# Two attention blocks with backward: a recurrence that keeps its state in one tile and stores wide rows, and a backward recurrence with regrouped heads, a fourth PSUM buffer and copies on ScalarE

## The chip, the cores and the metric

The kernel runs on one core of one Trainium2 chip. The metric is device time in microseconds (us). The kernel before took 9784.7 us (median of 4 runs, 9771.98 to 9796.26).

Engine names are as in the profile: PE is TensorE, PEld its weight loads, DVE VectorE, ACT ScalarE, POOL GpSimd, SP the queue that issues most DMAs. "Granted clock" (PEclk) is the share of the full TensorE clock that the throttle let through. PSUM tiles are the ones that matmuls write; an "evacuation" copies such a tile out on DVE or ACT.

## The reference

The forward function mixes two attention blocks over 2048 tokens of width 512; the kernel returns its output and the gradients for 11 of its inputs.

```python
g = sigmoid((x * gate_w).sum(-1, keepdims=True))
a = A(x)         # 32 heads of 16, shared k and v, full softmax
b = B(x)         # the part that this change touches
out = g * a + (1 - g) * b

# B: a recurrence over 64 segments of 32 tokens with 8 memory rows
mem = mem0
for s in range(64):
    h = concat([mem, x[s*32:(s+1)*32]])        # 40 rows
    q, k, v = h @ Wq, h @ Wk, h @ Wv           # 32 heads of 128
    p = softmax(mask(q @ k.T * scale))         # 40 x 40 in each head
    o = (p @ v) @ Wo
    mem = o[:8]                                # what the next segment needs
    outs.append(o[8:])
# reference(): jax.vjp of all this for grad_out
```

## The kernel before

One program does, in this order: attention A forward and backward (untouched); the B forward recurrence ("forward"); the combination with the gate; the B backward recurrence ("backward"); and four passes that accumulate the weight gradients of Wq, Wk, Wv and Wo ("dW", passes q, k, v, o). The two recurrences cannot overlap their steps: step s+1 needs the memory rows (or their gradient) of step s.

The forward step, cut:

```python
for s_ in range(NS):                                     # 64 steps
    hT = sp.tile([P, 4, TB], BF16, name="hT")            # TB = 40 = 32 tokens + 8 memory rows
    nc.vector.tensor_copy(out=hT[:, :, 0:LB], in_=xT[:, :, s_ * LB:(s_ + 1) * LB])
    nc.vector.tensor_copy(out=hT[:, :, LB:TB], in_=memT_cur[:])
    qT_s = project("qT", Wq, 0); kT_s = project("kT", Wk, 1)   # 128 matmuls each, ps_proj
    # ... scores, softmax, vT, transposes ...
    nc.scalar.dma_start(PT_all[s_], PT[:])               # nothing reads PT_all
    # ... o of this step into columns slot3*40.. of oT3 [128, 32 heads, 128] ...
    oT_s = oT3[:, :, slot3 * TB:(slot3 + 1) * TB]
    nc.sync.dma_start(oT_all[s_], oT_s)                  # 128 x 32 runs of 80 B
    # ps_m = Wo^T o for the 8 memory rows (128 matmuls, ps_memT)
    nc.vector.tensor_copy(out=memT_next[:], in_=ps_m[:]) # copied again into hT in the next step
```

The backward step, cut. `R` copies are evacuations of 128x128 transposes; heads alternate between partitions 0-39 (even) and 64-103 (odd):

```python
psA = pool("bb_psA", bufs=3, PSUM); psB = pool("bb_psB", bufs=2, PSUM)   # psC: three tags, one bank each
# load qT_s, kT_s into [128, 32, 64] (80 B runs), vT_s, P2 twice; transpose d(out) into dobT
doT_s = Wo^T dob                                # 128 matmuls ps_doT, three evacuations
for gi, (h0, h1) in enumerate(HGRPS):           # heads 0-11, 12-23, 24-31
    # ps_dP = doT . vT, head h at partition 64 * (h % 2)
    for par in range(2):                        # 4 DVE operations on 6 (or 4) heads
        prod = ps_dP * P2; delta = sum(prod); tsub = ps_dP - delta; dS2 = tsub * SCALE_B * P2
do_R = transposes_R2(doT_s)                     # two 128x1024 copies, both on DVE
dvT_s = grad_T(do_R, P2)                        # per group: two half tiles of psA, evacuated on ACT and DVE
dh_part(0, WvT, dvT_s)                          # 128 matmuls, ps_dhT
k_R = transposes_R2(kT_s); q_R = transposes_R2(qT_s)
# dST = transposes of dS2; dkT = grad_T(q_R, dS2); dh_part(1, WkT); dqT = grad_T(k_R, dST); dh_part(2, WqT)
nc.scalar.copy(out=dh_f[:], in_=ps_dh[:, 0])                                   # the "tail"
nc.vector.tensor_tensor(out=dh_f[:], in0=dh_f[:], in1=ps_dh[:, 1], op=ALU.add)
nc.vector.tensor_tensor(out=dhT_s[:], in0=dh_f[:], in1=ps_dh[:, 2], op=ALU.add)
nc.vector.tensor_copy(out=dmemT_new[:], in_=dhT_s[:, :, LB:TB])   # copied again into dobT next step
```

The framework orders each engine's instructions when it builds the program, so the source order above is not the order on DVE or PE.

The softmax here doesn't subtract the row's maximum and nothing guards it: scores larger than these inputs give would overflow.

## Time and profile before

| stage | from - to, us | length | per step (64) | granted clock |
|---|---|---|---|---|
| attention A | 0 - 4148 | 4148 | | 0.96 |
| forward | 4148 - 6030 | 1882 | 29.4 | 0.76 |
| combine, weights | 6030 - 6219 | 189 | | 0.69 |
| backward | 6219 - 8364 | 2145 | 33.5 | 0.76 |
| dW | 8364 - 9776 | 1412 | | 0.84 |

The table is read from the busy times of stretches of the trace, kernel before. Columns: stretch in us from the start, its length, busy us of each engine with its number of instructions, then granted clock, mean busy share of the DMA engines, GB/s.

```profile
core 0: us, PE busy (x) PEld busy (x) DVE busy (x) ACT busy (x) POOL busy (x), PEclk, DMA share, GB/s
0.00:4148.00 4148.00, 3596.12 (x93133) 3253.67 (x93134) 2891.06 (x7880) 2655.93 (x5199) 296.81 (x533) 0.96 0.40 141
4148.00:6030.00 1882.00, 1562.08 (x46923) 1481.02 (x46924) 662.68 (x1170) 446.39 (x768) 8.40 (x21) 0.76 0.50 56
6030.00:6219.00 189.00, 55.80 (x959) 48.08 (x957) 61.96 (x146) 36.23 (x56) 14.99 (x26) 0.69 0.60 167
6219.00:8364.00 2145.00, 1722.45 (x46584) 1556.83 (x46584) 1237.08 (x3197) 269.80 (x768) 200.29 (x311) 0.76 0.40 70
8364.00:9776.00 1412.00, 991.51 (x25348) 954.07 (x25348) 840.00 (x1234) 238.64 (x233) 351.01 (x608) 0.84 1.03 86
```

Forward first. The waits of PE in the forward stage, kernel before: who waited for whom, us in total, times, longest.

```profile
engine line waited for: us in total, times, longest us
PE ps_proj L52 <- issue: 236.3, 103, 5.7
PE ps_oT L668 <- DVE oT L673: 15.0, 20, 0.7
...
```

"issue" means that PE waited for nothing that the profile shows: no semaphore. A loss of 236 us to nothing is worth asking about. The same view of stretches, in steps of 1 us over one forward step (same columns as above), kernel before; the oT_all store was issued at 4225.88:

```profile
4228.00:4229.00 1.00, 1.00 (x43) 1.00 (x41) 0.00 (x0) 0.00 (x0) 0.00 (x0) 0.50 1.66 78
4229.00:4230.00 1.00, 1.00 (x40) 1.00 (x38) 0.10 (x1) 0.00 (x0) 0.00 (x0) 0.50 2.18 22
4230.00:4231.00 1.00, 1.00 (x30) 1.00 (x28) 0.27 (x2) 0.00 (x0) 0.00 (x0) 0.50 1.76 36
4231.00:4232.00 1.00, 1.00 (x36) 1.00 (x33) 0.00 (x0) 0.00 (x0) 0.00 (x0) 0.50 1.91 39
4232.00:4233.00 1.00, 1.00 (x36) 1.00 (x33) 0.00 (x0) 0.56 (x1) 0.00 (x0) 0.50 1.72 20
...
4234.00:4235.00 1.00, 0.11 (x2) 0.03 (x2) 0.66 (x1) 0.00 (x0) 0.00 (x0) 1.00 0.27 3
4235.00:4236.00 1.00, 0.00 (x0) 0.00 (x0) 0.00 (x0) 0.00 (x0) 0.00 (x0) 1.00 0.19 3
4236.00:4237.00 1.00, 0.49 (x16) 0.49 (x16) 0.00 (x0) 0.00 (x0) 0.00 (x0) 0.77 0.04 1
```

The last two columns tell it. For some 6 us the DMA engines are fully busy (the share adds the time of packets, and passes 1 here) while they move only 20 to 80 GB/s: that is the store in runs of 80 B. At 4234 to 4236.5 PE stands still. The queue list of the page, kernel before, has a queue of kind "instruction" (packets, MB, share):

```profile
q8 instruction: 1668, 27.33, 1.3%
```

That is 16.4 KB a packet. The Trainium skill, page "Runtime: NRT & Kernel Launch", section "Instruction fetch mechanics", says that an engine's instructions come by DMA in blocks of 16 KiB, and calls the cost mostly hidden. The packet size agrees. PE has 426969 instructions in this trace, 256 for each of the 1668 packets.

Backward next. The chain of work that ended last, in order of time, kernel before (start, us, what, times). One step's DVE part runs from the first `prod` to WvT's matmuls:

```profile
7000.62 0.41 DVE prod L876
...
7010.73 0.34 DVE prod L876
7011.09 0.33 DVE dS L884
7011.44 0.32 DVE delta L878
7011.78 0.42 DVE dvT_s L816
...
7012.24 0.29 PE ps_dT L894 x4
7012.53 4.06 PE ps_dhT L52 x115
```

From 7000.62 to 7012.46 (where PE starts the 115 matmuls) are 11.84 us in which DVE is busy for 11.12 us and PE for 6.86. The chain passes through softmax operations (prod, delta, tsub, dS) until the last evacuation of dvT on DVE, then PE takes over. Groups of instructions by shape in the backward stage, kernel before (count, busy us, mean ns, idle before):

```profile
L876 DVE TENSOR_TENSOR prod<-ps_dP,P 40x240 f32<-40x240 f32 x256 | 103.8, 405 | 12.3 <-PE ps_dP L868 4.2
L876 DVE TENSOR_TENSOR prod<-ps_dP,P 40x160 f32<-40x160 f32 x128 | 41.3, 323 | 4.0
L828 DVE COPY do_R<-ps_tr 128x1024 bf16<-128x1024 bf16 x128 | 87.4, 683 | 2.0
```

240 elements take 405 ns, 160 take 323, and an R copy 683.

### The profile page before, as it was taken

The numbers are of one execution on the slowest core, as the hardware profiler recorded it, in microseconds if no ns is written. First come the engines' busy times: TensorE is split into PE (matmuls) and PEld (weight loads), VectorE is DVE, ScalarE is ACT, GpSimd is POOL, SyncE is SP. The second block draws the span as 40 slices with busy tenths as digits, with TensorE's granted clock in tenths as the row PEclk, the third lists the DMA queues.
The fourth block names the chain that finished last, engine by engine and source line by source line (L and its number), as shares of the span: only waits on it lengthen the run. The fifth ranks groups of instructions, "written<-read, shape, count | busy, mean of one in ns | idle before, by whom it ended". The sixth has DMA issues, their size and how long they took to land.

```text
span 9776.5 us, 461191 instructions
## 1 busy us (share of the span) xinstructions
PE 7928.0 (81%) x212940; PEld 7293.7 (75%) x212940; DVE 5692.8 (58%) x13627; ACT 3647.0 (37%) x7023; POOL 871.5 (9%) x1498
## 2 busy tenths in 40 slices
PE   5999998799999998488888886678887887477677
PEld 5778877788888898377777875577777777477667
DVE  2555555599999998033333333455555555466556
ACT  3666666477777776022222221211111111111111
POOL 0000000000000000000000000000000000122221
PEclk9999999999999999577777777777777777689888
DMA  2444444244444443244554545534343433999996
GB/s 88 166 166 167 168 166 166 100 140 141 141 141 142 141 143 118 99 57 56 55 57 57 57 56 92 117 69 69 69 71 69 72 70 67 106 84 71 105 87 61
DMA packets 2184111, 994.17 MB, mean 102 GB/s; under 512 B 1926144, under 2 KB 1970336, under 8 KB 2179104
## 3 DMA queue, kind: packets, MB, share of 16 engines
q1 hardware_dynamic: 1312320, 561.59, 30.8%
q10 hardware_dynamic: 772832, 108.85, 10.4%
q0 software_dynamic: 97024, 294.21, 8.9%
q8 instruction: 1668, 27.33, 1.3%
q14 instruction: 267, 2.19, 0.1%
HBM read 494.58 MB, written 464.59 MB: 98 GB/s over the span
## 4 chain that ended last, share of the span: by engine, by line
PE 46%; DVE 15%; issue 7%; ACT 6%; DMA 4%; SPq 2%; ACTq 1%; POOL 0%; another core or an unknown queue 0%; DVEq 0%; POOLq 0%
PE ps_dhT L52 8%; PE ps_proj L52 7%; PE ps_acc L1074 4%; PE ps_T L421 3%; ACT dsub L410 3%; PE ps_VK L417 2%; PE ps_ob L575 2%; PE ps_memT L680 2%; PE ps_doT L52 2%; PE ps_dP L68 2%; PE ps_acco L1062 2%; DVE dST L423 2%; SPq L1017 2%; DVE prod L876 2%; DVE delta L878 1%
## 5 line engine op out<-in xcount | busy, mean ns | idle before, releaser
L410 ACT ACTIVATE dsub<-ps_dP,delta 128x512 bf16<-128x512 f32 x2048 | 1296.7, 686 | 128.8 <-DVE dS L412 64.0
L275 ACT ACTIVATE E_t<-ps_S 128x1024 bf16<-128x1024 f32 x1024 | 1039.1, 1020 | 556.9 <-PE ps_S L68 555.6
L68 PE MATMUL ps_dP<-VT16x,dOTg 128*128 128x57 bf16 (+1 forms) x18432 | 929.6, 190 | 50.5 <-ACT dsub L410 50.1
L281 DVE COPY ET<-ps_T 128x1024 bf16<-128x1024 bf16 x1024 | 708.2, 692 | 432.3 <-PE ps_T L279 432.3
L423 DVE COPY dST<-ps_T 128x512 bf16<-128x512 bf16 x2048 | 863.5, 422 | 42.7 <-PE ps_T L421 41.9
L421 PE MATMUL ps_T<-ident,dS 128*128 128x128 bf16 x8192 | 786.9, 218 | 0.0
L279 PE MATMUL ps_T<-ident,E_t 128*128 128x128 bf16 x8192 | 713.8, 220 | 76.9 <-ACT E_t L275 75.3
L68 PEld LDWEIGHTS <-dOTg 128*128 128x128 bf16 x18432 | 722.5, 97 | 68.5 <-issue 67.3
L412 DVE TENSOR_TENSOR dS<-dsub,E_b 128x512 bf16<-128x512 bf16 x2048 | 770.5, 418 | 0.5 <-ACT dsub L410 0.4
L1074 PE MATMUL ps_acc<-R,hr 120*128 120x68 bf16 (+1 forms) x16896 | 612.6, 198 | 125.6 <-issue 120.0
L415 PE MATMUL ps_VK<-dOs_R,E_b 128*128 128x16 bf16 x8192 | 707.0, 170 | 0.7 <-DVE dKacc L429 0.2
L68 PE MATMUL ps_S<-KT16x,QTg 128*128 128x57 bf16 (+1 forms) x18432 | 701.0, 190 | 0.0
L1074 PEld LDWEIGHTS <-hr 120*128 120x128 bf16 x16896 | 588.0, 102 | 139.8 <-issue 133.2
L417 PE MATMUL ps_VK<-Qs_R,dS 128*128 128x16 bf16 x8192 | 665.4, 170 | 30.2
L68 PEld LDWEIGHTS <-QTg 128*128 128x128 bf16 x18432 | 629.3, 98 | 0.0
L279 PEld LDWEIGHTS <-E_t 128*128 128x128 bf16 x8192 | 466.4, 97 | 171.5 <-ACT E_t L275 115.3
L415 PEld LDWEIGHTS <-E_b 128*128 128x128 bf16 x8192 | 560.2, 96 | 42.6 <-issue 0.2
L417 PEld LDWEIGHTS <-dS 128*128 128x128 bf16 x8192 | 503.4, 96 | 70.4 <-DVE dS L412 70.1
L1037 ACT COPY R<-ps_tr 128x1024 bf16<-128x1024 bf16 x176 | 175.7, 1013 | 947.7 <-PE ps_tr L1032 727.8
L426 PE MATMUL ps_dQ<-Ka_R,dST 128*128 128x16 bf16 x8192 | 515.2, 171 | 1.1 <-DVE dST L423 0.8
L421 PEld LDWEIGHTS <-dS 128*128 128x128 bf16 x8192 | 475.2, 96 | 0.1
L283 PE MATMUL ps_o<-Va_R,ET 128*128 128x16 bf16 x8192 | 367.8, 171 | 75.3 <-DVE ET L281 68.0
(256 smaller groups left out, 14598.0 us busy)
## 6 DMA issues: line engine op xcount, KB each, us to landing
E_all<-E_t SPq DMA_DIRECT2D x256, 512.0 KB
E_all<-E_t POOLq DMA_DIRECT2D x256, 512.0 KB, 2.9
E_b<-E_all SPq DMA_DIRECT2D x256, 512.0 KB
E_b<-E_all POOLq DMA_DIRECT2D x256, 512.0 KB, 3.7
qT_all<-qT_s SPq DMA_DIRECT2D x64, 320.0 KB
kT_all<-kT_s ACTq DMA_DIRECT2D x64, 320.0 KB
vT_all<-vT_s SPq DMA_DIRECT2D x64, 320.0 KB
oT_all<-oT SPq DMA_DIRECT2D x64, 320.0 KB
```

The lines of the kernel that those rows point to most:

```text
L52: nc.tensor.matmul(out, lhsT=lhsT, rhs=rhs, start=(j == 0), stop=(j == last), **kw)
L68: nc.tensor.matmul(out[:, pos:pos + n], lhsT=lhsT, rhs=rhs[:, pos:pos + n], start=(j == 0), stop=(j == last), **kw)
L275: nc.scalar.activation(E_kh, ps_S[:], ACT.Exp, scale=SCALE_A, accum_out=l_kh[:])
L279: nc.tensor.transpose(ps_T[:, kb, :], E_kh[:, kb * P:(kb + 1) * P], ident[:])
L281: nc.vector.tensor_copy(out=ET[:], in_=ps_T[:])
L410: nc.scalar.activation(dsub[:], ps_dP[:], ACT.Identity, bias=delta[:, qt, h:h + 1])
L412: nc.vector.tensor_tensor(out=dS[:], in0=dsub[:], in1=E_t[:, c0:c0 + SUBW], op=ALU.mult)
L415: nc.tensor.matmul(ps_VK[:, 0, kk, :], lhsT=E_t[:, c0 + kb * P:c0 + (kb + 1) * P], rhs=dOs_R[:, qt, h * DA:(h + 1) * DA], start=True, stop ...
L417: nc.tensor.matmul(ps_VK[:, 1, kk, :], lhsT=dS[:, kb * P:(kb + 1) * P], rhs=Qs_R[:, qt, h * DA:(h + 1) * DA], start=True, stop=True)
L421: nc.tensor.transpose(ps_T[:, kb, :], dS[:, kb * P:(kb + 1) * P], ident[:])
L423: nc.vector.tensor_copy(out=dST[:], in_=ps_T[:])
L1074: nc.tensor.matmul(ps[:, pos:pos + n], lhsT=Hs[ci][:, cc * P:(cc + 1) * P], rhs=Rs[ci][0:KCH * TB, hc * D + pos:hc * D + pos + n], start=( ...
```

## The change

It aims at three things: small DMA packets (the oT_all store, its loads in dW, a dead PT_all store), copies between steps, and the backward's DVE chain. The diff, cut to its core:

```diff
@@ forward
-    oT_all = dram.tile([NSEG, P, HB, TB], ...)
+    oT_all = dram.tile([(NSEG + 2) // 3, P, HB, P], ...)
-    memT_cur -> copied into hT each step
+    hT_next: ps_memT is evacuated straight into the next step's hT
-        nc.scalar.dma_start(PT_all[s_], PT[:])
-        nc.sync.dma_start(oT_all[s_], oT_s)
         if slot3 == 2 or s_ == NS - 1:
+            nc.sync.dma_start(oT_all[s_ // 3], oT3[:])       # 1 MB in 8 KB rows, every third step
@@ backward
-    psA bufs=3
+    psA bufs=4        # ps_dbT and ps_dhR moved to other tags
+    # heads 0-11 and 24-27 at partitions 0-39, 12-23 and 28-31 at 64-103
+    GSUB = {0: [(0, 12, 0)], 1: [(12, 24, 64)], 2: [(24, 28, 0), (28, 32, 64)]}
     transposes_R2:
-            nc.vector.tensor_copy(out=dstR[...hg...], in_=ps_t[:])
+            if hg == 0: nc.vector.tensor_copy(...)
+            else:       nc.scalar.copy(...)
-        nc.sync.dma_start(qT_s[:, :, 0:TB], qT_all[s_]); nc.scalar.dma_start(kT_s[:, :, 0:TB], kT_all[s_])
+        four DMAs each for q and k, by head block, on both queues
     softmax backward, grad_T, dST:
-        for par in range(2): ...            # 24 DVE operations, six dvT tiles
+        for (hlo, hhi, b) in GSUB[gi]: ...  # 16 DVE operations, four dvT tiles
     tail:
-        ACT copy, two DVE adds, two DVE copies
+        nc.vector.tensor_reduce(out=dh_f[:], in_=ps_dh.rearrange("p m cc t -> p cc t m"), axis=AX.X, op=ALU.add)
+        nc.vector.tensor_copy(out=dobT_next[:, :, LB:TB], in_=dh_f[:, :, LB:TB])
@@ dW
+                if m == "o": one dma_start(T3[:], oT_all[ch[0] // 3])   # in place of three with 80 B runs
```

More of the change, by code (lines that the diff above doesn't have):

```diff
@@ L526, in phase_B_fwd @@
     vT_all = dram.tile([NSEG, P, HB, TB], BF16, name="vT_all")
-    oT_all = dram.tile([NSEG, P, HB, TB], BF16, name="oT_all")
-    PT_all = dram.tile([NSEG, TB, HB, TB], BF16, name="PT_all")
+    oT_all = dram.tile([(NSEG + 2) // 3, P, HB, P], BF16, name="oT_all")
     P_all = dram.tile([NSEG, TB, HB, TB], BF16, name="P_all")
@@ L550, in phase_B_fwd @@
     psf1 = octx.enter_context(tc.tile_pool(name="b_ps1", bufs=1, space=bass.MemoryType.PSUM))
-    memT_cur = sp.tile([P, 4, MB], BF16, name="memT_cur")
-    nc.sync.dma_start(memT_cur[:], memT_all[0])
+    hT_next = sp.tile([P, 4, TB], BF16, name="hT")
+    nc.sync.dma_start(hT_next[:, :, LB:TB], memT_all[0])
     ob_queue = []
@@ L598, in phase_B_fwd @@
     for s_ in range(NS):
-        hT = sp.tile([P, 4, TB], BF16, name="hT")
+        hT = hT_next
         nc.vector.tensor_copy(out=hT[:, :, 0:LB], in_=xT[:, :, s_ * LB:(s_ + 1) * LB])
-        nc.vector.tensor_copy(out=hT[:, :, LB:TB], in_=memT_cur[:])
         def project(wname, W, eng_off):
@@ L681, in phase_B_fwd @@
                                  start=(h == 0), stop=(h == HB - 1))
-        memT_next = sp.tile([P, 4, MB], BF16, name="memT_cur")
-        nc.vector.tensor_copy(out=memT_next[:], in_=ps_m[:])
-        nc.scalar.dma_start(memT_all[s_ + 1], memT_next[:])
-        memT_cur = memT_next
+        hT_next = sp.tile([P, 4, TB], BF16, name="hT")
+        nc.vector.tensor_copy(out=hT_next[:, :, LB:TB], in_=ps_m[:])
         if slot3 == 2 or s_ == NS - 1:
@@ L692, in phase_B_fwd @@
     octx.close()
-    return dict(qT_all=qT_all, kT_all=kT_all, vT_all=vT_all, oT_all=oT_all, PT_all=PT_all,
+    return dict(qT_all=qT_all, kT_all=kT_all, vT_all=vT_all, oT_all=oT_all,
                 P_all=P_all, memT_all=memT_all, memR_all=memR_all, b_hbm=b_hbm)
@@ L755, in phase_B_bwd @@
     qT_all, kT_all, vT_all, oT_all = bst["qT_all"], bst["kT_all"], bst["vT_all"], bst["oT_all"]
-    P_all, PT_all, memR_all = bst["P_all"], bst["PT_all"], bst["memR_all"]
+    P_all, memR_all = bst["P_all"], bst["memR_all"]
     db_hbm = cst_["db_hbm"]
@@ L801, in phase_B_bwd @@
     rp = octx.enter_context(tc.tile_pool(name="bb_rp", bufs=3, side="right"))
-    psA = octx.enter_context(tc.tile_pool(name="bb_psA", bufs=3, space=bass.MemoryType.PSUM))
+    psA = octx.enter_context(tc.tile_pool(name="bb_psA", bufs=4, space=bass.MemoryType.PSUM))
     psB = octx.enter_context(tc.tile_pool(name="bb_psB", bufs=2, space=bass.MemoryType.PSUM))
     psC = octx.enter_context(tc.tile_pool(name="bb_psC", bufs=1, space=bass.MemoryType.PSUM))
-    dmemT_cur = sp.tile([P, 4, MB], BF16, name="dmemT_cur")
-    nc.vector.memset(dmemT_cur[:], 0.0)
+    dobT_next = sp.tile([P, 4, TB], BF16, name="dobT")
+    nc.vector.memset(dobT_next[:, :, LB:TB], 0.0)
     zr = sp1.tile([MB, D], BF16, name="zr")
@@ L818, in phase_B_bwd, with hbase, hpair @@
     TPAD = 64
+    def hbase(h):
+        return 0 if (h < 12 or 24 <= h < 28) else 64
+    def hpair(h):
+        if h < 12:
+            return h, 0
+        if h < 24:
+            return h - 12, 1
+        if h < 28:
+            return 12 + (h - 24), 0
+        return 12 + (h - 28), 1
+    PAIR_BLOCKS = [((slice(0, 12), 0), (0, 12)), ((slice(0, 12), 1), (12, 24)),
+                   ((slice(12, 16), 0), (24, 28)), ((slice(12, 16), 1), (28, 32))]
+    GSUB = {0: [(0, 12, 0)], 1: [(12, 24, 64)], 2: [(24, 28, 0), (28, 32, 64)]}
     def transposes_R2(srcTp, name):
@@ L825, in transposes_R2 @@
                 pr = hg * 8 + j
-                nc.tensor.transpose(ps_t[:, j, :], srcTp[:, 2 * pr:2 * pr + 2, :].rearrange("e a t -> e (a t)"),
-                                    ident[:])
-            nc.vector.tensor_copy(out=dstR[:, hg * 8:(hg + 1) * 8, :], in_=ps_t[:])
+                nc.tensor.transpose(ps_t[:, j, :], srcTp[:, pr, :, :].rearrange("e a t -> e (a t)"), ident[:])
+            if hg == 0:
+                nc.vector.tensor_copy(out=dstR[:, hg * 8:(hg + 1) * 8, :], in_=ps_t[:])
+            else:
+                nc.scalar.copy(out=dstR[:, hg * 8:(hg + 1) * 8, :], in_=ps_t[:])
         return dstR
@@ L832, in phase_B_bwd @@
         s_ = NS - 1 - si
-        qT_s = ld.tile([P, HB, TPAD], BF16, name="qT_s")
-        kT_s = ld.tile([P, HB, TPAD], BF16, name="kT_s")
+        qT_s = ld.tile([P, HB // 2, 2, TPAD], BF16, name="qT_s")
+        kT_s = ld.tile([P, HB // 2, 2, TPAD], BF16, name="kT_s")
         vT_s = ld.tile([P, HB, TB], BF16, name="vT_s")
-        nc.gpsimd.memset(qT_s[:, :, TB:TPAD], 0.0)
-        nc.gpsimd.memset(kT_s[:, :, TB:TPAD], 0.0)
-        nc.sync.dma_start(qT_s[:, :, 0:TB], qT_all[s_])
-        nc.scalar.dma_start(kT_s[:, :, 0:TB], kT_all[s_])
+        nc.gpsimd.memset(qT_s[:, :, :, TB:TPAD], 0.0)
+        nc.gpsimd.memset(kT_s[:, :, :, TB:TPAD], 0.0)
+        for bi, ((psl, slot), (hlo, hhi)) in enumerate(PAIR_BLOCKS):
+            eng = nc.sync if bi % 2 == 0 else nc.scalar
+            eng.dma_start(qT_s[:, psl, slot, 0:TB], qT_all[s_][:, hlo:hhi, :])
+            eng.dma_start(kT_s[:, psl, slot, 0:TB], kT_all[s_][:, hlo:hhi, :])
         nc.sync.dma_start(vT_s[:], vT_all[s_])
@@ L846, in phase_B_bwd @@
         nc.sync.dma_start(drow[pb:pb + LB, :], db_hbm[s_ * LB:(s_ + 1) * LB, :])
-        ps_db = psC.tile([P, 4, TB], BF16, name="ps_dbT", tag="dbT")
+        ps_db = psC.tile([P, 4, TB], BF16, name="ps_dbT", tag="m1")
         for cc in range(4):
@@ L850, in phase_B_bwd @@
                                 ident[pb:pb + LB, pb:pb + LB], tile_position=(pb, 0))
-        dobT = sp.tile([P, 4, TB], BF16, name="dobT")
+        dobT = dobT_next
         nc.vector.tensor_copy(out=dobT[:, :, 0:LB], in_=ps_db[:, :, 0:LB])
-        nc.vector.tensor_copy(out=dobT[:, :, LB:TB], in_=dmemT_cur[:])
-        doT_s = sp.tile([P, HB, TPAD], BF16, name="doT_s")
-        nc.gpsimd.memset(doT_s[:, :, TB:TPAD], 0.0)
+        doT_s = sp.tile([P, HB // 2, 2, TPAD], BF16, name="doT_s")
+        nc.gpsimd.memset(doT_s[:, :, :, TB:TPAD], 0.0)
         for gi, (h0, h1) in enumerate(HGRPS):
@@ L859, in phase_B_bwd, with doT_h @@
                 mm_acc(nc, ps[:, h - h0, :], [(WoT[:, cc, h * EB:(h + 1) * EB], dobT[:, cc, :]) for cc in range(4)])
-            evac(gi, doT_s[:, h0:h1, 0:TB], ps[:, 0:h1 - h0, :])
+            for k, (hlo, hhi, b) in enumerate(GSUB[gi]):
+                psl, slot = hpair(hlo)[0], hpair(hlo)[1]
+                evac(gi + k, doT_s[:, psl:psl + (hhi - hlo), slot, 0:TB], ps[:, hlo - h0:hhi - h0, :])
+        def doT_h(h):
+            pr, sl = hpair(h)
+            return doT_s[:, pr, sl, 0:TB]
         delta = sp.tile([P, HB], F32, name="delta")
@@ L863, in phase_B_bwd @@
         for gi, (h0, h1) in enumerate(HGRPS):
-            ng = h1 - h0
             ps = psA.tile([P, 12, TB], F32, name="ps_dP", tag="p12")
             for h in range(h0, h1):
-                b = 64 * (h % 2)
-                nc.tensor.matmul(ps[b:b + TB, h - h0, :], lhsT=doT_s[:, h, 0:TB], rhs=vT_s[:, h, :],
+                b = hbase(h)
+                nc.tensor.matmul(ps[b:b + TB, h - h0, :], lhsT=doT_h(h), rhs=vT_s[:, h, :],
                                  start=True, stop=True, tile_position=(0, b))
-            for par in range(2):
-                b = 64 * par
-                hs = slice(h0 + par, h1, 2)
-                ss = slice(par, ng, 2)
-                npar = len(range(h0 + par, h1, 2))
-                prod = sp1.tile([P, 6, TB], F32, name="prod")
-                nc.vector.tensor_tensor(out=prod[b:b + TB, 0:npar, :], in0=ps[b:b + TB, ss, :],
-                                        in1=P2[b:b + TB, hs, :], op=ALU.mult)
-                nc.vector.tensor_reduce(out=delta[b:b + TB, hs], in_=prod[b:b + TB, 0:npar, :], axis=AX.X,
+            for (hlo, hhi, b) in GSUB[gi]:
+                nh = hhi - hlo
+                s0 = hlo - h0
+                prod = sp1.tile([P, 12, TB], F32, name="prod")
+                nc.vector.tensor_tensor(out=prod[b:b + TB, 0:nh, :], in0=ps[b:b + TB, s0:s0 + nh, :],
+                                        in1=P2[b:b + TB, hlo:hhi, :], op=ALU.mult)
+                nc.vector.tensor_reduce(out=delta[b:b + TB, hlo:hhi], in_=prod[b:b + TB, 0:nh, :], axis=AX.X,
@@ L879, in phase_B_bwd @@
                                         op=ALU.add)
-                tsub = sp1.tile([P, 6, TB], F32, name="tsub")
-                nc.vector.tensor_tensor(out=tsub[b:b + TB, 0:npar, :], in0=ps[b:b + TB, ss, :],
-                                        in1=delta[b:b + TB, hs].unsqueeze(2).to_broadcast([TB, npar, TB]),
+                tsub = sp1.tile([P, 12, TB], F32, name="tsub")
+                nc.vector.tensor_tensor(out=tsub[b:b + TB, 0:nh, :], in0=ps[b:b + TB, s0:s0 + nh, :],
+                                        in1=delta[b:b + TB, hlo:hhi].unsqueeze(2).to_broadcast([TB, nh, TB]),
@@ L883, in phase_B_bwd, with grad_T @@
                                         op=ALU.subtract)
-                nc.vector.scalar_tensor_tensor(out=dS2[b:b + TB, hs, :], in0=tsub[b:b + TB, 0:npar, :],
-                                               scalar=SCALE_B, in1=P2[b:b + TB, hs, :],
+                nc.vector.scalar_tensor_tensor(out=dS2[b:b + TB, hlo:hhi, :], in0=tsub[b:b + TB, 0:nh, :],
+                                               scalar=SCALE_B, in1=P2[b:b + TB, hlo:hhi, :],
                                                op0=ALU.mult, op1=ALU.mult)
-        def grad_T(wname, lhsR2, rhs2, out_all):
+        def grad_T(wname, lhsR2, rhs2, out_all, groups=None):
@@ L888, in grad_T @@
             dst = sp.tile([P, HB, TB], BF16, name=f"{wname}_s", tag=wname)
             for gi, (h0, h1) in enumerate(HGRPS):
-                ps_par = [psA.tile([P, 12, TB], F32, name=f"ps_dT{par}", tag="p12") for par in range(2)]
-                for h in range(h0, h1):
-                    par = h % 2
-                    b = 64 * par
-                    nc.tensor.matmul(ps_par[par][:, (h - h0) // 2, :], lhsT=lhsR2[b:b + TB, h // 2, :],
-                                     rhs=rhs2[b:b + TB, h, :], start=True, stop=True, tile_position=(b, 0))
@@ L896, in grad_T @@
-                for par in range(2):
-                    npar = len(range(h0 + par, h1, 2))
-                    evac(gi + 1 + par, dst[:, h0 + par:h1:2, :], ps_par[par][:, 0:npar, :])
+                subs = GSUB[gi]
+                pss = [psA.tile([P, 12, TB], F32, name=f"ps_dT{k}", tag="p12") for k in range(len(subs))]
+                for k, (hlo, hhi, b) in enumerate(subs):
+                    for h in range(hlo, hhi):
+                        pr, _ = hpair(h)
+                        nc.tensor.matmul(pss[k][:, h - hlo, :], lhsT=lhsR2[b:b + TB, pr, :],
+                                         rhs=rhs2[b:b + TB, h, :], start=True, stop=True, tile_position=(b, 0))
@@ L899, in grad_T @@
+                for k, (hlo, hhi, b) in enumerate(subs):
+                    evac(gi + 1 + k, dst[:, hlo:hhi, :], pss[k][:, 0:hhi - hlo, :])
             nc.sync.dma_start(out_all[s_], dst[:])
@@ L913, in phase_B_bwd @@
         dST = sp1.tile([P, HB, TB], BF16, name="dST")
-        for hg in range(2):
-            ps_par = [psB.tile([P, 8, 64], BF16, name=f"ps_dST{par}", tag="tr") for par in range(2)]
-            for j in range(16):
-                h = hg * 16 + j
-                par = h % 2
-                b = 64 * par
-                nc.tensor.transpose(ps_par[par][b:b + TB, j // 2, 0:TB], dS2[b:b + TB, h, :],
-                                    ident[b:b + TB, b:b + TB], tile_position=(b, b))
-            for par in range(2):
-                b = 64 * par
-                nc.vector.tensor_copy(out=dST[b:b + TB, hg * 16 + par:(hg + 1) * 16:2, :],
-                                      in_=ps_par[par][b:b + TB, 0:8, 0:TB])
+        for gi, (h0, h1) in enumerate(HGRPS):
+            subs = GSUB[gi]
+            pss = [psB.tile([P, 12, 64], BF16, name=f"ps_dST{k}", tag="tr") for k in range(len(subs))]
+            for k, (hlo, hhi, b) in enumerate(subs):
+                for h in range(hlo, hhi):
+                    nc.tensor.transpose(pss[k][b:b + TB, h - hlo, 0:TB], dS2[b:b + TB, h, :],
+                                        ident[b:b + TB, b:b + TB], tile_position=(b, b))
+            for k, (hlo, hhi, b) in enumerate(subs):
+                nc.vector.tensor_copy(out=dST[b:b + TB, hlo:hhi, :], in_=pss[k][b:b + TB, 0:hhi - hlo, 0:TB])
         dkT_s = grad_T("dkT", q_R, dS2, dkT_all)
@@ L930, in phase_B_bwd @@
         dh_f = sp.tile([P, 4, TB], F32, name="dh_f")
-        nc.scalar.copy(out=dh_f[:], in_=ps_dh[:, 0])
-        nc.vector.tensor_tensor(out=dh_f[:], in0=dh_f[:], in1=ps_dh[:, 1], op=ALU.add)
+        nc.vector.tensor_reduce(out=dh_f[:], in_=ps_dh[:].rearrange("p m cc t -> p cc t m"), axis=AX.X,
+                                op=ALU.add)
+        dobT_next = sp.tile([P, 4, TB], BF16, name="dobT")
+        nc.vector.tensor_copy(out=dobT_next[:, :, LB:TB], in_=dh_f[:, :, LB:TB])
         dhT_s = sp.tile([P, 4, TB], BF16, name="dhT_s")
-        nc.vector.tensor_tensor(out=dhT_s[:], in0=dh_f[:], in1=ps_dh[:, 2], op=ALU.add)
-        dmemT_new = sp.tile([P, 4, MB], BF16, name="dmemT_cur")
-        nc.vector.tensor_copy(out=dmemT_new[:], in_=dhT_s[:, :, LB:TB])
-        dmemT_cur = dmemT_new
-        ps_r = psC.tile([TB, D], BF16, name="ps_dhR", tag="misc")
+        nc.scalar.copy(out=dhT_s[:], in_=dh_f[:])
+        ps_r = psB.tile([TB, D], BF16, name="ps_dhR", tag="tr")
         for cc in range(4):
@@ L1014, in issue_loads @@
                 T3 = ldp.tile([P, HB, P], BF16, name="T3")
+                if m == "o":
+                    (nc.sync if ci % 2 == 0 else nc.scalar).dma_start(T3[:], oT_all[ch[0] // 3])
+                    T3s.append(T3)
+                    continue
                 for j, st_ in enumerate(ch):
```

## The prediction

> **What bounds it now.** The timeline's 9776 us: attention A to 4148 (untouched); B forward 4148-6030 (1882 us, 64 steps of 29.3); combine and weights to 6219; B backward 6219-8366 (2147 us, 64 steps of 33.5); four dW passes to 9776 (q, k, v, o).
> Forward is a serial PE chain. The waits table gives PE 236 us idle before ps_proj with "issue" as releaser, 103 times, 3.7 us a step. In 1-us windows the oT_all store (4096 runs of 80 B) lasts about 7 us at DMA share near 1.9 but 20-40 GB/s, then PE stands for 2-5 us inside ps_proj. The Trainium skill, "Runtime: NRT & Kernel Launch", Instruction fetch mechanics, says instructions come by DMA in 16 KiB blocks; the queue table agrees (1668 "instruction" packets, 27.3 MB, 16.4 KB each). I read the stalls as instructions delayed behind the store. After them the granted clock is often 0.5 (36 matmuls/us, against 47).
> Backward alternates: for about 12 us DVE is the chain (24 softmax-backward operations of 0.32-0.40 us, three R copies of 0.69, dvT evacuations), then about 17 us of PE, then a 1.5 us tail (ACT copy, two adds, two copies) before ps_doT.
> dW is limited by 80 B loads (DMA share 1.66) and their stalls (PE "issue" 148 us).
>
> **Changes, costed.**
> Forward: the store becomes 8 KB rows every third step: the 3.7 us should go. Copy hT L601: 0.2 us. Better clock: 0.3 us, an estimate. About 4 us x 64 = -250 us (200 to 310).
> Backward: DVE: 24 operations become 16. From 240 elements = 0.40 us and 160 = 0.32, I estimate 480 = 0.66, so 9.0 us becomes 7.8, plus 8 hops of 0.03; half of the R copies go to ACT (one or two within the chain); an extra doT copy is 0.3. Net -2 us. Tail: one reduce (0.66, estimated) and one copy (0.19) against 1.5: -0.5. Against: heads no longer alternate row groups. ps_dT runs alternating at about 20 ns each; forward's ps_oT, same shape, one row group, at 28-38. The skill's "TensorE: Matmul & The Clock Gate", Part 3 (The mechanism), says weight loads overlap matmuls only when the row group differs, which fits. 96 matmuls: +1 to 1.5 us of PE, some 0.9 on the path, dP included. The last dvT tile still waits for the last tsub despite a fourth psA buffer, so WvT's matmuls stay behind the DVE chain. The q/k loads keep 80 B packets, in eight DMAs. Net -1.6 us a step, -100 us (-220 to +30).
> dW: only pass o changes. It takes 329 us from its first transpose (9447); without DMA limits, 7.3 supers of 31 us, start and output make about 265: -65. Its loads also delay the end of pass v (ACT held 46 us behind them): -30. Together -95 us (-50 to -130).
>
> Sum about -445: **9335 us, 80% range 9180 to 9500**. Chances: faster by over 2% 0.96, within 2% 0.035, slower 0.005.
>
> **What would show it.** Forward step 25-25.5 us; "issue" before ps_proj under 40 us. Backward step 31-32.5; softmax operations of 480 elements near 0.66; ps_dT dearer per matmul. Pass o about 265 us; passes q and k unchanged.
>
> **What would make it wrong.** Stalls not caused by the store; q and k loads bursting together and starving PE in backward; the scheduled order on ACT or DVE letting WvT's matmuls start earlier (up to 4 us a step) or holding evacuations behind DMA waits.

## The result

| | before | after |
|---|---|---|
| median, us | 9788.0 (13 runs) | 9057.4 (8 runs) |
| ratio, 95% interval | | 0.9252 [0.9242, 0.9261] |
| forward, us | 1882 | 1546 |
| backward, us | 2145 | 1842 |
| dW, us | 1412 | 1338 |

A ratio is the mean time of one kernel's runs over the mean of the other's of the same rounds, so it is not quite the ratio of the medians quoted. The kernel gained 731 us where 450 had been forecast; the measured time lies below the predicted range.

The stretches, kernel after (columns as before):

```profile
core 0: us, PE busy (x) PEld busy (x) DVE busy (x) ACT busy (x) POOL busy (x), PEclk, DMA share, GB/s
0.00:4149.00 4149.00, 3594.06 (x93132) 3251.54 (x93132) 2890.90 (x7879) 2655.91 (x5199) 296.80 (x533) 0.96 0.40 141
4149.00:5695.00 1546.00, 1475.22 (x46899) 1407.51 (x46900) 650.93 (x1106) 446.50 (x768) 8.39 (x21) 0.84 0.18 65
5695.00:5875.00 180.00, 53.92 (x989) 46.27 (x987) 61.79 (x146) 36.23 (x56) 14.95 (x26) 0.71 0.60 175
5875.00:7717.00 1842.00, 1580.16 (x46584) 1465.38 (x46580) 1014.39 (x2240) 420.62 (x767) 196.90 (x311) 0.86 0.50 81
7717.00:9055.00 1338.00, 989.96 (x25348) 954.62 (x25348) 840.56 (x1233) 239.47 (x233) 342.88 (x586) 0.84 0.88 93
```

The waits of PE in the forward stage, kernel after:

```profile
...
PE ps_proj L52 <- issue: 6.0, 16, 0.7
...
```

The store now, in 1-us stretches, kernel after; it was issued at 4723.12:

```profile
4724.00:4725.00 1.00, 1.00 (x43) 1.00 (x41) 0.00 (x0) 0.00 (x0) 0.00 (x0) 0.50 1.07 426
4725.00:4726.00 1.00, 1.00 (x44) 1.00 (x42) 0.00 (x0) 0.00 (x0) 0.00 (x0) 0.50 0.99 393
4726.00:4727.00 1.00, 1.00 (x34) 1.00 (x32) 0.29 (x2) 0.00 (x0) 0.00 (x0) 0.50 0.39 156
4727.00:4728.00 1.00, 1.00 (x35) 1.00 (x33) 0.00 (x0) 0.00 (x0) 0.00 (x0) 0.50 0.08 33
```

One MB in rows of 8 KB passes in under 3 us at up to 426 GB/s, and PE stays at 1.00. The chain of one backward step, kernel after:

```profile
6719.29 0.65 DVE prod L893
...
6725.24 0.33 DVE prod L893
6725.58 0.67 DVE dS L901
6726.27 0.31 DVE delta L895
6726.59 0.24 DVE dvT_s L811
...
6726.87 3.14 PE ps_dhT L52 x100
```

From 6719.29 to 6726.87 are 7.58 us in place of 11.84 (the chain's view ends with 100 of a run of 104). The two runs are not the same matmuls: before's 115 begin with the 14th of WvT's 128, after's 104 with the 25th. Counted alike, at the last 104, the start moved from 12.34 to 7.58 us after the first prod (medians of the 64 steps, counted in the traces), by 4.8 us, and the whole step became 4.7 us shorter. The groups, kernel after:

```profile
L893 DVE TENSOR_TENSOR prod<-ps_dP,P 40x480 f32<-40x480 f32 x128 | 83.3, 651 | 3.1 <-PE ps_dP L887 1.0
L893 DVE TENSOR_TENSOR prod<-ps_dP,P 40x160 f32<-40x160 f32 x128 | 41.2, 322 | 4.0
L840 ACT COPY do_R<-ps_tr 128x1024 bf16<-128x1024 bf16 x64 | 64.8, 1012 | 112.6 <-PE ps_tr L836 112.6
L838 DVE COPY do_R<-ps_tr 128x1024 bf16<-128x1024 bf16 x64 | 43.1, 673 | 0.0
```

480 elements take 651 ns; the prediction had estimated 660. The durations were right. What was wrong was which of them lie ahead of WvT's matmuls, as the experiments show.

### The profile page after: what moved, and what is told of

Same layout as the page of the kernel before. It is cut to its first block, busy times and chain, and to the rows that moved or that the text cites. A ratio compares the mean times of both kernels' runs of the same rounds, so it can differ in the third digit from the quotient of the medians.

```text
span 9055.7 us, 460371 instructions
## 1 busy us (share of the span) xinstructions
PE 7693.3 (85%) x212940; PEld 7125.3 (79%) x212940; DVE 5458.6 (60%) x12603; ACT 3798.7 (42%) x7023; POOL 859.9 (9%) x1476
## 4 chain that ended last, share of the span: by engine, by line
PE 62%; DVE 12%; ACT 11%; issue 6%; DMA 5%; SPq 2%; ACTq 1%; POOL 0%; DVEq 0%; POOLq 0%
PE ps_dhT L52 8%; PE ps_proj L52 7%; PE ps_T L279 7%; PE ps_acc L1092 5%; ACT E_t L275 4%; PE ps_T L421 3%; PE ps_S L68 3%; ACT dsub L410 3%; PE ps_VK L417 3%; PE ps_doT L52 2%; PE ps_memT L676 2%; PE ps_ob L574 2%; PE ps_dP L68 2%; DVE dST L423 2%; PE ps_acco L1080 2%
## 5 line engine op out<-in xcount | busy, mean ns | idle before, releaser
L1092 PE MATMUL ps_acc<-R,hr 120*128 120x68 bf16 (+1 forms) x16896 | 625.5, 200 | 106.5 <-issue 100.6
```

What stands on the lines that cost most here:

```text
L1092: nc.tensor.matmul(ps[:, pos:pos + n], lhsT=Hs[ci][:, cc * P:(cc + 1) * P], rhs=Rs[ci][0:KCH * TB, hc * D + pos:hc * D + pos + n], start=( ...
```

## The experiments

All 14 results were correct against the reference. "Stage" times are read from the profiled run of each kernel between the same instructions: forward from the first ps_proj to the last ps_memT, backward from the first ps_doT to the last dh_f. They compare kernels across calls better than totals do: in the third call the kernel before itself ran at 9716.41 us, where it took 9775 to 9787 in the others. The same backward took 1831 to 1842 us in four kernels (bwd_only, after_80B, after, after_again), so a stage difference of under some 12 us says nothing.

My theories were: in the forward the 80 B store starves PE; in the backward a fourth PSUM buffer lets WvT's matmuls start early. The rival for the forward was the saved copies; for the backward, the copies on ACT or the wider operations.

### Do the stages add up?

`fwd_only` is the kernel before with the forward and dW of after; `bwd_only` is the kernel before with the backward of after.

> Before with the forward and the dW pass of after, backward as before. If the three stages add up: forward 1882 to about 1547 us, dW 1410 to about 1340, so 9788 - 410 = about 9375 us (9350 to 9400), and the backward stays at 2147 us. If the stages lean on each other (for example, a backward that gains because the forward left something better), it is over 9430.

> Before with the backward of after alone. Additive: backward 2147 to about 1843 us, so 9788 - 303 = about 9485 us (9460 to 9510), forward still 1882 us with about 230 us of PE 'issue' before ps_proj. Rival, that part of the backward's gain came from the forward or from HBM traffic that the forward no longer makes: over 9550.

Measured: fwd_only 9363.27 us, ratio 0.9574, forward 1544, backward 2143. bwd_only 9459.36 us, ratio 0.9676, forward 1869, backward 1831. The two gains, 0.0426 and 0.0324, sum to 0.0750, against 0.0748 for the whole change. The stages are independent, and can be studied one by one.

### The store alone

`store_only` is the kernel before with only this:

```diff
-    oT_all = dram.tile([NSEG, P, HB, TB], ...)
+    oT_all = dram.tile([(NSEG + 2) // 3, P, HB, P], ...)
-        nc.sync.dma_start(oT_all[s_], oT_s)
+            nc.sync.dma_start(oT_all[s_ // 3], oT3[:])      # every third step; dW reads it so
```

> Before with nothing changed but the oT_all store (22 of 1 MB in 8 KB rows in place of 64 of 80 B runs) and its loads in dW; memT copy, PT_all store, backward as before. Theory, that the 80 B store starved PE of instructions and the stalls also pulled the granted clock down: nearly all of the forward's and dW's gain, about 9395 us (9370 to 9420), 'issue' before ps_proj under 20 us, forward clock about 0.84. Rival, that the saved copies and the PT_all store carry a good part: 9500 or more.

Measured: 9389.55 us, ratio 0.9596; forward 1569 us, "issue" before ps_proj 3.3 us, forward clock 0.84, PE busy 1483 us against 1562. The theory holds: 313 of the forward's 336 us come from the store. 233 us of them are the standing time; some 79 us more are PE busy time, for the same matmuls at a higher clock. The saved copies and the PT_all store are the remaining 23 us or so (1569 against 1546).

### The store put back

`after_80B` is the kernel after with one dead store a step into a scratch tensor that nothing reads:

```diff
+        nc.sync.dma_start(oT_scr[s_], oT_s)       # 80 B runs, [NSEG, P, HB, TB]
```

> After plus one dead store a step in the forward: oT in 80 B runs into a scratch tensor that nobody reads, as before's oT_all store; dW still reads the wide copy. Theory, that the store starves PE's instruction fetch and drags the clock down: the forward goes back to about 1860 us, 'issue' before ps_proj to about 230 us, forward clock from 0.84 to about 0.76, the other stages unchanged; about 9057 + 315 = 9370 us (9330 to 9400). Rival, that it was the wait of some reader or the copies: under 9100 us.

Measured: 9337.39 us, ratio 0.9605; forward 1832 us, clock 0.78; backward 1836, unchanged. PE's wait in the forward, of this kernel:

```profile
PE ps_proj L52 <- issue: 217.4, 89, 5.4
```

No instruction waits for the data of this store, yet PE's unexplained waiting is back. So the small-packet store causes it: shown. That the stalls are late instruction blocks can be counted in the kept traces. Number PE's instructions in order of time and take the number modulo 256, the instructions of one packet: of the 64 waits of over 1 us before ps_proj in the forward of before, 61 end at one and the same place of 256; in after_80B all 64 do, at the same place again. In both, PE went on a median 2.2 us after a packet of the instruction queue had landed. After and store_only have no such wait. So PE stands at the edges of instruction blocks. How the store holds a block up is not shown; the trace has a packet's time on the DMA engines (up to 3.5 us in the forward of before, up to 1.9 in that of after), but not when it was asked for. (It came out 33 us under the middle of what I expected; the kernel before was faster too.)

### The fourth PSUM buffer

`after_psA3` is after with `bufs=3` for psA; `before_psA4` is before with `bufs=4` (ps_dbT and ps_dhR moved, as in after).

> After with 3 psA buffers in place of 4 in the backward (one PSUM bank left empty). Theory, that the fourth buffer lets the dvT tiles recycle while the two ps_dP tiles are still held, so that WvT's matmuls start some 3 us before the DVE chain ends: backward steps 2 to 3.5 us longer, 9190 to 9280 us, WvT's matmuls again after the last tsub. Rival, that the fewer and wider DVE operations and the ACT copies made the gain: within 40 us of after, under 9100.

> Before with 4 psA buffers in place of 3 in the backward (ps_dbT and ps_dhR moved to other tags to make room), nothing else. If the fourth buffer alone is worth 2 to 3.5 us a step: 9560 to 9660 us. If it needs the wider groups too (before makes six dvT tiles of half size, after four), it gains under 1 us a step: 9720 or more.

Measured: after_psA3 9104.91 us, ratio 0.9309, backward 1878. before_psA4 9733.5 us, ratio 0.9942, backward 2088. The fourth buffer is worth 36 us to the kernel after and 57 to the kernel before, under 1 us a step. In the kernel after my theory fell: with three buffers WvT's last 104 matmuls still start 7.58 us after the first prod, just as in after (lines of the timeline of after_psA3):

```profile
6709.94 0.64 DVE L893 TENSOR_TENSOR prod<-ps_dP,P 40x480 f32<-40x480 f32 x1
...
6717.52 3.52 PE L52 MATMUL ps_dhT<-dvT_s,WvT 128*128 128x40 bf16 x104 [0.49 <-DVE dvT_s L811]
```

In the kernel before it held in part: with four buffers the last 104 start 11.26 us after the first prod, with three 12.34 (medians of 64 steps, from the traces). These 1.1 us are about the 0.9 us a step that before_psA4 gains, but 23 of the 24 softmax operations still stand ahead.

### The copies on ACT

`after_R_dve` puts all six R copies of a step back on DVE:

```diff
-            if hg == 0: nc.vector.tensor_copy(...)
-            else:       nc.scalar.copy(...)
+            nc.vector.tensor_copy(out=dstR[:, hg * 8:(hg + 1) * 8, :], in_=ps_t[:])
```

> After with all six R copies of a step on DVE, as before. Two of the three moved copies lie within the DVE chain (0.69 us each), so 9057 + 64 x 1.4 = about 9145 us (9100 to 9190); if DVE has slack there, under 9075.

Measured: 9240.77 us, ratio 0.944, backward 2011: 169 us or 2.6 us a step, the largest single part, and more than the two copies of 0.69 us that I had counted. The chain of one step of this kernel:

```profile
6702.59 0.65 DVE prod L890
...
6711.80 0.34 DVE dvT_s L811
...
6712.18 3.63 PE ps_dhT L52 x104
```

WvT's matmuls now start 9.59 us after the first prod, 2.0 us later than in after. The rest comes after them. Two more kernels split it. `after_doR_act` keeps only do_R's second copy on ACT; `after_kqR_act` only k_R's and q_R's.

> After with only do_R's second half on ACT; k_R's and q_R's copies all on DVE as before. All six on DVE cost 184 us (2.9 us a step). If the cost is that do_R's second copy queues behind softmax operations on DVE while ps_dT of dvT waits for it, most comes back here: 9057 + about 60 = 9115 us (9090 to 9140). If each of the three moved copies is worth the same DVE time: 9057 + 123 = 9180.

> After with only do_R's copies all on DVE; the second halves of k_R and q_R on ACT. The counterpart: if do_R's place in the DVE order is the cost, about 9057 + 120 = 9175 us (9150 to 9210); if each copy is worth its share of DVE time, 9057 + 61 = 9118.

Measured: after_doR_act 9123.15 us, ratio 0.9386, backward 1902; after_kqR_act 9163.26 us, ratio 0.9427, backward 1953. In their own call the same backward as after's, in after_80B, took 1836. So putting back do_R's copy costs 117 us, or 1.8 us a step; putting back k_R's and q_R's together costs 66. Their sum of 183 is near the 169 for all three, and the totals lie where the theory of do_R's place put them (9115 and 9175), not where equal shares would (9180 and 9118). Their ratios would put them higher, because before was faster in this call, so the stage times carry this reading. With do_R's copy on ACT the start is again 7.58 us after the first prod (6710.66 to 6718.24), without it 9.60 (6710.22 to 6719.82). do_R's second copy costs more than its 0.69 us because ps_dT of dvT cannot run without it, and while it queues on DVE, more softmax operations get ahead of the dvT evacuation that WvT waits for: 15 of the 16 have started when the last 104 begin, against 11 in after. q_R's copy is short of the same thing: after WvT's matmuls, the transposes of dS wait for it.

### The wider groups

`after_parity` has after's forward, fourth buffer, ACT copies and tail, but before's alternating heads: 24 softmax operations, six dvT tiles, and one DMA each for q and k.

> After with the backward's head grouping of before (heads alternate between the two row groups, 24 DVE operations, six dvT tiles, q and k loads in one DMA each), but its fourth psA buffer, its ACT copies and its short tail kept. My sum of DVE times says the regrouping saves 1.4 us of DVE a step, and nothing on PE; so 9057 + 64 x 1.4 = about 9150 us (9120 to 9180). If the row group alternation were worth what I predicted (0.9 us a step), about 9090. If the number of tiles matters for the early start of WvT's matmuls, 9250 or more.

Measured: 9173.99 us, ratio 0.9376, backward 1944: 102 us, or 1.6 us a step. DVE's own busy time in this backward is 90 us higher than in after (1104 against 1014), which is the 1.4 us a step of my sum. WvT's last 104 start 9.25 us after the first prod, 1.7 us later than in after (medians, from the traces). The q and k loads changed with it, so their share is not separated here.

### The tail

`after_tail` has before's five operations between ps_dhT and ps_doT.

> After with the tail of before (ACT copy, two DVE adds, two DVE copies between ps_dhT and ps_doT). The tail is on the chain: 1.5 us against 0.95, so +0.55 us a step, about 9092 us (9075 to 9110).

Measured: 9080.42 us, ratio 0.9276, backward 1857: 15 us, or 0.23 us a step, under half of what I had said. In the totals it is 23 us, with an interval of some 17 us either way. The trace has the other half: the next step's ps_doT starts 0.72 us later after the first prod than in after, but its run is 0.43 us shorter, since the four ps_dhR transposes no longer stand inside it (medians). The 15 us are also little more than the 12 us by which the same backward differs between kernels.

### The row groups

`after_alt` issues the ps_dT matmuls of heads 0-11 and 12-23 (and of 24-27 and 28-31) in turn, so that successive matmuls use the two row groups (partitions 0-39 and 64-103) alternately, as in before's source. `after_again` is the kernel after in the same call.

```diff
-        for k, (hlo, hhi, b) in enumerate(subs):
-            for h in range(hlo, hhi): matmul(pss[k][:, h - hlo, :], ...)
+        for j in range(n):                      # (0-11 with 12-23), then (24-27 with 28-31)
+            for k, (hlo, hhi, b) in enumerate(subs): matmul(pss[k][:, j, :], ...)
```

> The changed kernel again, as the reference for the run beside it and for the chip: 9030 to 9075 us as before, backward about 1840 us, or lower where this chip's kernel before is also lower.

> After with only the order of the ps_dT matmuls changed: heads 0-11 and 12-23 (and 24-27 with 28-31) are issued alternately, so that successive matmuls again use the two row groups in turn, as in before. My prediction charged the loss of this alternation at 1 to 1.5 us of PE a step, 0.9 on the path. If that were so: about 58 us faster than after, under 9010. If alternation is worth nothing at 40 columns, the matmuls keep their about 20 ns each, and the time is that of after or a little longer, since the first evacuation of each pair waits for twice as many matmuls: 9040 to 9130.

Measured: after_again 9055.51 us, ratio 0.9264; after_alt 9077.05 us, ratio 0.9288, 22 us slower; but the backward, where the edit is, took 1845.5 us against 1842.2, and most of the rest lies in dW, which it does not touch. So the edit is worth nothing that can be seen here. Sixteen ps_dT matmuls in the timeline, first after_again, then after_alt, both in stretches at clock 1.0:

```profile
6701.33 0.49 PE L913 MATMUL ps_dT<-dS,q_R 40*128 40x40 bf16 x16
```

```profile
6727.56 0.37 PE L912 MATMUL ps_dT<-dS,q_R 40*128 40x40 bf16 x16
```

Taking off the 0.18 us of one matmul, 15 follow in 0.31 us (21 ns each) and in 0.19 us (13 ns each). The starts of single matmuls in the traces say why: where the order alternates, they come in pairs, 3 ns and 22 ns apart, and in one row group every 25 ns, at full clock. So alternation is faster, which fits the Trainium skill ("TensorE: Matmul & The Clock Gate", Part 3, "The mechanism"): it says that weight loads overlap matmuls only when the row group differs. But by these gaps the first run above already alternates in part, and in after_alt the 32 matmuls of dvT still start 25 ns apart, as in after. The built order is not the source order. On all 96 matmuls of a step after_alt saves some 0.2 us, so it is a weak test of the charge; the traces of before and after are the better one (see below).

### The same treatment for the other passes

`better1` takes after and applies the wide store to the other three passes of dW: the backward gathers dqT, dkT and dvT of three steps in tiles of [128, 32, 128] and stores them every third step; a few small backward tiles are single-buffered for room.

```diff
-    dqT_all = dram.tile([NSEG, P, HB, TB], ...)              # also dkT_all, dvT_all
+    dqT_all = dram.tile([(NSEG + 2) // 3, P, HB, P], ...)
-            dst = sp.tile([P, HB, TB], ...); nc.sync.dma_start(out_all[s_], dst[:])
+            dst = d3t[:, :, slot * TB:(slot + 1) * TB]
+            if slot == 0: nc.sync.dma_start(out_all[s_ // 3], d3t[:])
```

> After with the same treatment for the other three dW passes: the backward gathers dqT, dkT and dvT of three steps in one tile and stores 1 MB in 8 KB rows every third step, and dW loads them so (some small backward tiles single-buffered to make room). If passes q, k and v are limited by their 80 B loads as pass o was (329 to 249 us from its first acc to the end), each shortens by about 70 us to about 265, so 9057 - 210 = about 8850 us (8780 to 8930). Rival, that they are bound by PE and DVE as well: over 8990.

Measured: 8819.99 us, ratio 0.9075 [0.906, 0.9091], against 0.9252 for after. Its dW stage:

```profile
7717.00:8815.00 1098.00, 930.19 (x25373) 898.60 (x25369) 840.46 (x1233) 241.75 (x233) 318.12 (x520) 0.91 0.34 119
```

1098 us against 1338, at a DMA share of 0.34 against 0.88 and a clock of 0.91 against 0.84; the backward stays at 1847. PE's waits without a semaphore before ps_acc fall from 100.6 to 17.6 us. It beats both kernels. (This is the call in which the kernel before took 9716 us. Against after, better1 gains 237 us by its own time and some 173 by the ratios; the stage, 240 us shorter, agrees with the time.)

## Why the prediction was wrong

The direction and the mechanism in forward and dW were right; the sum was some 280 us too small. By stage:

| stage | predicted, us | measured, us |
|---|---|---|
| forward | -250 (200 to 310) | -336 |
| backward | -100 (-220 to +30) | -303 |
| dW | -95 (-50 to -130) | -74 |

**Forward: right mechanism, one term too small.** "The 3.7 us should go" was right: 230 us of standing time went. "Better clock: 0.3 us, an estimate" was the mis-sized term. PE's busy time fell by 87 us for the same matmuls, 1.4 us a step, and store_only shows 79 of them with the store alone. I had priced only the waiting, although the stretches before showed the clock at 0.5 in ps_proj beside the stalls. The copies gave 23 us where I had said 13.

**Backward: the step that failed** is this: "The last dvT tile still waits for the last tsub despite a fourth psA buffer, so WvT's matmuls stay behind the DVE chain." They do not. In before 23 of 24 softmax operations have started when WvT's long run begins; in after 11 of 16 have, and five follow under PE's matmuls. I had counted DVE's total work and taken its end as WvT's start. WvT waits for the last dvT evacuation, and where that stands in DVE's list depends on when do_R is ready. So the early start that I had listed among the risks is what happened. It came from do_R's copy on ACT (2.0 us later in after_R_dve) and from the wider groups (1.7 us later in after_parity). The buffer gives nothing in after (after_psA3), though 1.1 us in before (before_psA4). The three sum to the 4.8 us by which the start moved, with the buffer's part taken in before and the others in after.

The terms of the backward, per step of 64, by undoing one part of after at a time:

| term | predicted, us | measured, us |
|---|---|---|
| R copies on ACT | 0.7 to 1.4 | 2.6 |
| wider groups, with their loads | 1.4, less 0.9 on PE | 1.6 |
| fourth psA buffer | 0 | 0.6 |
| tail | 0.5 | 0.23 |

They sum to 5.0, against 4.7 for the whole backward.

**The row group charge** (0.9 us a step) was a second wrong step. One row group does cost more for each matmul (25 ns against pairs of 3 and 22). But the premise that before alternates and after does not is true of the source only. In the built order before's dvT matmuls start 25 ns apart too, and after's of dkT alternate in part. Mean gaps at full clock, before and after: dvT 25.4 and 27.6 ns, dkT 18.1 and 17.5, dqT 16.9 and 21.0 (gaps over 60 ns left out). By an estimate from these, the 96 matmuls became dearer by some 0.2 us, where I had charged 1 to 1.5. I had compared ps_dT at "about 20 ns" with ps_oT of the forward at 28 to 38. The ps_oT run at 38 (24 matmuls in 1.06 us from 4223.74) ran at a clock of 0.5 and contained a wait for an evacuation. Like was not compared with like.

**dW: right within its range.** Pass o takes 280 us from its first transpose to the end (8776 to 9056), predicted 265, before 329. The end of pass v gained about 24 us, predicted 30. Passes q and k were unchanged, as predicted.

The granted clock in the backward rose from 0.76 to 0.86, and the busy time of its long matmul runs (ps_doT and ps_dhT) fell by 54 us, 0.85 us a step, for the same count. That was in no term of mine. No run here changes the clock alone, so what share of each part above is clock stays open.

## What to carry to other kernels

Look at how long a DMA keeps the engines busy per byte before calling it "off the path": a store nobody waits for can still stop an engine whose waits have no semaphore. When one engine serves two chains, do not compare totals; list the operations that stand ahead of the one that releases the next engine, since moving one copy that feeds it away can bring it forward by several places. And where a stall is removed beside a low clock, price the matmuls after it too.

## What the Trainium skill lacked or had wrong

- "Runtime: NRT & Kernel Launch", section "Instruction fetch mechanics", calls the fetch of 16 KiB blocks mostly hidden. Beside a store in 80 B runs PE stood 236 us in 1882 without a semaphore, and 217 us when only such a store was put back. The waits stand at block edges (61 of 64 at one place modulo 256 instructions). The page has no word on DMA traffic delaying the fetch.
- "DMA: Bandwidth & Descriptors" gives 512 B as the least size for full rate, with no measured trn2 rate for a store far below it. Here a store of 320 KB in 80 B runs held the engines for about 6 us at 20 to 80 GB/s in most 1-us stretches, where 1 MB in 8 KB rows passed in under 3 us at up to 426 GB/s.
- "TensorE: Matmul & The Clock Gate", Part 3, says that weight loads overlap matmuls only when the row group differs. Its measured speedups for row tiling are at N=512. Here matmuls of 40 rows and 40 columns started 25 ns apart in one row group, and in pairs 3 and 22 ns apart alternating, at full clock.
